# Seven products instead of the plain second product for the third pair of batch 0, with the sums of w2 made earlier

## The chip, the cores and the metric

The kernel runs on one core of one Trainium2 chip. The metric is the device time of one execution in microseconds, given as the median of several runs. Lower is better.

## The reference

Four batches, eight heads, 768 time steps, 48 channels a head. An outer-product recurrence with a forget gate is followed by a mixer over tokens (low rank 32) and channels (384 to 1536 to 384):

```
f = sigmoid(f_logit)
state = f[t,:,None] * state + outer(k[t], v[t])      # per batch and head
y[t]  = q[t] @ state
x = y with the heads side by side                     # 768 x 384 per batch
u = x + (x^T U V)^T                                   # U 768x32, V 32x768
out = u + relu(u @ w_ch1) @ w_ch2                     # 384x1536, 1536x384
```

All is float32, apart from the weights, which arrive as float64 and are turned into float32 on the chip.

## The kernel before

**Units and batches.** Attention is worked in 16 units: unit `n` is one pair of heads of batch `n // 4` (HP = 4 pairs a batch). The front of a unit prepares its operands: `gates` (transpose L748 on VectorE, sigmoid L849 on ScalarE), `keep` (scan L854 and small operations L859 to L864), `keys` (L748 and L791, into kz), `read_back` (scan L872) and `queries` (L748 and L791, into qT). Its rear uses them: `kept` (transposes of kz on TensorE, L980), `states` (products L1001, copied by ScalarE L1008), `scan` (L1023 on VectorE, copied by GpSimd L1027), `scores` (L953, masked into A by VectorE L966), `read` (products L1039) and `inner` (products with A, L1057, then a copy into x by ScalarE, L1063).

**The mixer.** When a batch's attention is done, its `Mixer` follows: `low_rank` and `added_up` (L184, L197), `mix_blocks` (products L214, and an add of each pair of blocks into x by VectorE), `turn` (transposes of x, L288, copied by L289), then for each of three pairs `a` of token blocks the first products (`ch1`, L300, with a relu L335 into z) and the second products. A pair is two blocks of 128 tokens.

**Second products in two ways.** Batch 0 uses plain ones (`ch2`, L352): for each of the two blocks, 12 products of 384 columns, in four pieces of three, with one add to x by VectorE at the end. The other batches use Winograd's form with seven products of quarters in place of eight: `sums_of` makes four sums of z's quarters on VectorE, and `seven` makes the products in steps 0 to 3 (two, two, two and one product, each of six matmuls of 192 columns, L386), with adds on VectorE. Step 1 multiplies by the second and third sums of w2's quarters, step 2 by the fourth and first, steps 0 and 3 by quarters of w2 themselves. Each step of a batch's last pair takes a tile of two PSUM banks ("big", three of them in turn), which the mix products and the turns also use. The float32 matmuls appear as two records each in the trace.

**The sums of w2.** `quarters` makes four sums once, with VectorE: three in tiles named zw, which hold batch 0's z before, and the fourth over a quarter of w2 itself, which the plain form still needs until batch 0's last second product.

**The order of work.** TensorE's order is the written one all through. Up to the fourth piece of batch 1's second phase the orders of VectorE and ScalarE are the written ones too; instructions that come later in the code are placed by a planner and can stand between these. `add` marks VectorE's adds as urgent. `steps` lists the pieces of attention by unit, and `attention` calls a `Fill` before each piece. `Fill` spreads a list of (cost, piece) evenly over a number of portions:

```
self.due += self.share
while self.pieces and self.pieces[0][0] / 2 <= self.due:
    cost, piece = self.pieces.pop(0)
    self.due -= cost
    piece()
```

The attention of batch 1 (from unit 5's `keep` on, 35 pieces) is filled with batch 0's second products of pairs 0 and 1, 16 plain pieces of equal cost. The pieces are, in order: keep 6, keys 6, two steps to (read 4, states 5, scan 5), read_back 6, queries 6, three steps to (inner 4, scores 5, kept 6), gates, keep and keys 7, two to (read 5, states 6, scan 6), three to (inner 5, scores 6, kept 7), read_back and queries 7, gates, keep and keys 8, two to (read 6, states 7, scan 7), three to (inner 6, scores 7, kept 8), read_back and queries 8, gates, keep and keys 9, two to (read 7, states 8, scan 8), inner 7.

`start_mixer(1, ...)` then mixes the second products of pair 2 into batch 1's mixer, in quarters of `after`: a quarter, `low_rank`, unit 9's read_back and queries, a quarter, `added_up`, a quarter, unit 10's gates and keep, `mix_blocks`, a quarter, the turns. The four sums of w2 follow, and then batch 1's first products.

Of the kernel before, what the change touches and what calls it, by code (L numbers as in the profile page):

```python
# [59 lines left out]
def weight_loader(nc, pool, dma):  # L60
# [5 lines left out]

    P = nc.NUM_PARTITIONS

    def load(dst, w, place=None):
# [9 lines left out]
        def start():  # L79
            raw = pool.tile([P, WP], U64, name="w_raw", bufs=RAW) if place is None else place()  # L80
            raw = T["raw"] = raw[0:rows, 0:n]
            dma.dma_start(out=shaped(raw), in_=w)

        def halves():
            y = pool.tile([P, WP], U32, name="w_y")[0:rows, 0:n]
            r = pool.tile([P, WP], I32, name="w_r", bufs=3)[0:rows, 0:n]
            words = T["raw"].bitcast(U32).rearrange("p (n two) -> p n two", two=2)
            lo, hi = words[:, :, 0], words[:, :, 1]

            f = y.bitcast(F32)  # L90
# [52 lines left out]
def by_rows(V, w, R):  # L143


    P, n = V.shape[0], w.shape[1] // V.shape[0]
    G = P // R
    return [
# [8 lines left out]
class Mixer:  # L157
# [6 lines left out]
    def __init__(self, tc, b, x, U, V, w1, w2, sums, ident, blocks, out, two, three, zp, ps_big, ps_mm, wide=False,  # L164
                 z_all=None, room=None, pair=0):
        nc = tc.nc
        P = nc.NUM_PARTITIONS
# [4 lines left out]
        NA = NCH // 2  # L172
        NI = NFC // 2
        HM = DM // 2
# [26 lines left out]
        def add(*args):  # L201

            with tc.high_priority(offset=AHEAD):
                nc.vector.tensor_tensor(*args)  # L204
# [18 lines left out]
        def mix_four():  # L223
            big = ps_big.tile([P, 2, 512], F32, name="pu", tag="big")
            pms = [big[:, s, :] for s in range(2)] + [ps_mm.tile([P, 512], F32, name="pu1", tag="mm") for _ in range(2)]
            for t, pm in enumerate(pms):
                mix_product(pm[:, 0:DM], t)
            add(x[:, 0:2, :], x[:, 0:2, :], big[:, :, 0:DM], ALU.add)
            for t in range(2, NG):
                add(x[:, t, :], x[:, t, :], pms[t][:, 0:DM], ALU.add)  # L230

        def mix_blocks():
            first = 0
            if b > 1 and sums is not None:
                mix_four()
                first = NG
            for t in range(first, NCH):
                mix(t)
# [120 lines left out]
        def part(a, r, c):  # L359
            return z[a, c][:, :, r * P : (r + 1) * P]  # L360

        def sums_of(a):
            for i in range(1, 5):
                if room and a >= pair and (a - pair) % 2 == 0:
                    s = room["S"][i - 1]
                else:
                    s = two.tile([P, WP], U64, name="w_raw", bufs=RAW).bitcast(F32)
                S[a, i] = s.rearrange("p (i t) -> p i t", t=P)
            add(S[a, 1], part(a, 1, 0), part(a, 1, 1), ALU.add)
            add(S[a, 2], S[a, 1], part(a, 0, 0), ALU.subtract)  # L370
            add(S[a, 3], part(a, 0, 0), part(a, 1, 0), ALU.subtract)
            add(S[a, 4], part(a, 0, 1), S[a, 2], ALU.subtract)

        W = {}

        def products(a, parts, *of):

            if 0 in parts:
                if a == NA - 1 and (not room or room["last"] == a - pair):
                    W["pm"] = ps_big.tile([P, 2, 512], F32, name="pw", tag="big")[:, 0]  # L380
                else:
                    W["pm"] = ps_mm.tile([P, 512], F32, name="pw", tag="mm")
            for n in parts:
                lhs, rhs = of[n]
                for i in range(NI):
                    nc.tensor.matmul(W["pm"][:, n * HM : (n + 1) * HM], lhsT=lhs[:, i, :], rhs=rhs[:, i, :],  # L386
                                     start=(i == 0), stop=(i == NI - 1))
            return W["pm"] if len(of) - 1 in parts else None

# [53 lines left out]
        def fewer(a):  # L443
# [51 lines left out]

            return [(FG * P * len(PRODUCTS[k : k + 2]), lambda k=k: two_of(k)) for k in range(0, len(PRODUCTS), 2)]

        def second(a):
            if sums is None:
                return [(2 * NFC * DM // NQ, lambda s=s, n=n: ch2(a, s, n)) for s in range(2) for n in range(NQ)]  # L500
            return [(2 * NFC * HM * (2 if step < 3 else 1) // 2, lambda step=step: seven(a, step))
                    for step in range(4)]

        def halved(a):

            if sums is None:
                return second(a)
            return [(NFC * HM, lambda step=step, n=n: seven(a, step, (n,)))
                    for step in range(4) for n in range(2 if step < 3 else 1)]

        def ready(a):
            return [] if sums is None else [(1, lambda: sums_of(a))]

        def first(a):
            return [(4 * NDC * 2 * P, lambda j=j: ch1(a, j)) for j in range(NI)]
# [5 lines left out]


        self.firsts = [p for j in range(NI) for a in range(NA) for p in [first(a)[j]]]
        self.seconds = [p for a in range(NA) for p in second(a)]
        self.main = first(0)
        for a in range(NA - 1):
            ahead = first(a + 1)
# [5 lines left out]
        self.sums_of_x = lambda a: [(1, lambda: sums_of_x(a))]  # L533


def quarters(nc, pool, w2):


    P = nc.NUM_PARTITIONS
    NI, HM = w2.shape[1] // 2, w2.shape[2] // 2  # L540
    q = {(i, j): w2[:, i * NI : (i + 1) * NI, j * HM : (j + 1) * HM] for i in range(2) for j in range(2)}
    sums = {4: q[0, 1]}
    sub = nc.vector.tensor_tensor

    def place():
        for i in range(1, 4):
            t = pool.tile([P, NI, 2 * P], F32, name="zw")
            sums[i] = t.rearrange("p i t -> p (i t)")[:, 0 : NI * HM].rearrange("p (i d) -> p i d", d=HM)

    return sums, [  # L550
        place,
        lambda: sub(sums[1], q[0, 1], q[0, 0], ALU.subtract),
        lambda: sub(sums[2], q[1, 1], sums[1], ALU.subtract),
        lambda: sub(sums[3], q[1, 1], q[0, 1], ALU.subtract),
        lambda: sub(sums[4], q[1, 0], sums[2], ALU.subtract),
    ]


def factored_path(ctx, tc, q, k, v, f_logit, moe_U, moe_V, moe_w_ch1, moe_w_ch2, out, ok):
# [4 lines left out]
    nc = tc.nc  # L564
    B, H, S, D = q.shape
    P = nc.NUM_PARTITIONS
# [3 lines left out]
    NBL = S // P  # L570
# [9 lines left out]
    W = TB * NB  # L580
# [35 lines left out]
    w1 = const.tile([P, NDC, FF], F32, name="w1")  # L616
    w2 = const.tile([P, NFC, DM], F32, name="w2")
# [99 lines left out]
    U = const.tile([P, NBL, R], F32, name="U")  # L717
    V = const.tile([P, (NBL * R + P - 1) // P, P], F32, name="V")
# [8 lines left out]
    def place():  # L727
        if not spare:
            t = zp.tile([P, NFC // 2, 2 * P], F32, name="zw").rearrange("p i t -> p (i t)").bitcast(U64)
            spare.extend([t[:, 0:WP], t[:, WP : 2 * WP]])  # L730
        return spare.pop(0)
# [3 lines left out]
        take_in(w1[:, :, i * P : (i + 1) * P], w1_rows[:, :, i * P : (i + 1) * P], place if i < FIRST else None)  # L735
        for i in range(NFC)
    ]
    sums, to_sum = quarters(nc, zp, w2)
    weights += [take_in(w2[:, i, :], moe_w_ch2[i * P : (i + 1) * P, :]) for i in range(NFC)]

    def backwards(t, first, n):
# [140 lines left out]
    x_tiles = {}  # L882

    def mixer(b):
        return Mixer(tc, b, x_tiles[b], U, V, w1, w2, sums if b else None, ident, blocks, out, two, three, zp, ps_big, ps_mm,
                     b == 0, z_all, room if b >= B - 2 else None, FEWER - (b - B + 2) * NCH // 4)


# [41 lines left out]
    plain = {n for of in PRODUCTS for _, n in of if n < 9}  # L930
# [222 lines left out]
    with tc.manual_schedule(engines={nc.vector.engine, nc.scalar.engine}):  # L1153
# [65 lines left out]
        m = mixer(0)  # L1219
# [35 lines left out]
        second = chain(front(HP, "gates", "keep", "keys", "read_back", "queries"), steps(HP, 2 * HP + 1))  # L1255
# [6 lines left out]
                next(second)()  # L1262
        for f in loads:
            f()
        n = len(m.seconds) // (NBL // 2)
        todo, after = m.seconds[:-n], m.seconds[-n:]

        attention(second, Fill(todo, 10 + 10 * HP - (len(start) + len(m.firsts) - 1 - EARLY)))
        n = 2 * HP + 2
        m = start_mixer(1, after, front(n - 1, "read_back", "queries"), front(n, "gates", "keep"))  # L1270
        for f in to_sum:
            f()
        pieces, fill = steps(n - 1, 3 * HP + 1), Fill(m.main, 10 * HP - 3)
        for _ in range(4):
            fill()
# [1 line left out]
    for b in range(2, B - 1):  # L1277
        if b > 2:
            pieces, fill = steps(b * HP + 1, (b + 1) * HP + 1), Fill(m.main, 10 * HP)
        after = m.after  # L1280
        attention(pieces, fill)
        m = start_mixer(b, after)
# [7 lines left out]
    todo = m.first(0) + m.ready(0) + m.halved(0)  # L1290
# [14 lines left out]
    todo = of(0, "sums_of_x") + of(0, "fewer")  # L1305
# [359 lines left out]
```

## Time and profile before

| | |
|---|---|
| median of three runs | 468.49 us (468.22 to 468.52) |
| the profiled execution | 467.36 us, span 465.5 us |
| granted TensorE clock | 0.998 |
| busy TensorE, VectorE, ScalarE, GpSimd | 455.7, 352.7, 165.8, 54.4 us |
| plain second products (L352), first to last start | 98.9 to 164.3 us |
| batch 0's pair 2, first to last record (L352) | 145.1 to 164.8 us |
| the four sums of w2 (L552 to L555) | 165.3 to 170.6 us |

A matmul's row in the profile gives its own duration, which overlaps its neighbours'; what a run of matmuls costs is read from the start of one group to the start of the next. VectorE's instructions overlap by less than 0.1 us. In the timelines a bracket gives the idle time ahead of an instruction and what ended it.

### The profile page before, as it was taken

How to read it: one execution, taken by the hardware profiler on the slowest of the kernel's cores; microseconds unless marked ns; L12 is line 12 of the kernel's file. 1: busy time of each engine (PE TensorE's matmuls, PEld its weight loads, DVE VectorE, ACT ScalarE, POOL GpSimd, SP SyncE). 2: the span in 40 equal slices, each digit the busy share in tenths (PEclk: the TensorE clock that was granted, in tenths of full speed). 3: DMA queues.
4: the chain of work that ended last, by engine and by line, in shares of the span. 5: the costliest groups of instructions: out<-in, count | busy, mean ns of one | idle time of the engine just before them, and what ended most of it. 6: DMA issues, size and time to landing. Idle time of an engine off the chain costs nothing.

```text
span 465.5 us, 13015 instructions
## 1 busy us (share of the span) xinstructions
PE 455.7 (98%) x5639; PEld 395.0 (85%) x5639; DVE 352.7 (76%) x581; ACT 165.8 (36%) x316; POOL 54.4 (12%) x60
## 2 busy tenths in 40 slices
PE   8999999999999999999999999999999999999996
PEld 6886888875666578999898888989989999999996
DVE  5777788979999676865774659977797877858642
ACT  6775776562333143323323223331412311112200
POOL 2002445634112001010001000020000000000000
PEclk9999999999999999999999999999999999999999
DMA  9948997577778504505534020100000000001001
GB/s 198 204 115 208 224 218 178 153 115 106 122 112 133 91 18 53 77 3 97 66 52 80 15 52 9 21 5 20 18 1 1 35 1 35 0 1 37 0 36 39
DMA packets 148343, 34.35 MB, mean 74 GB/s; under 512 B 136822, under 2 KB 146742, under 8 KB 148278
## 3 DMA queue, kind: packets, MB, share of 16 engines
q1 hardware_dynamic: 147478, 33.29, 36.2%
q8 instruction: 46, 0.75, 0.7%
q10 hardware_dynamic: 800, 0.15, 0.2%
q14 instruction: 19, 0.16, 0.1%
HBM read 28.70 MB, written 4.72 MB: 72 GB/s over the span
## 4 chain that ended last, share of the span: by engine, by line
PE 79%; DVE 12%; ACT 3%; issue 3%; DMA 2%; POOL 0%; SPq 0%; DVEq 0%; ACTq 0%; POOLq 0%
PE pw L386 25%; PE pz L300 21%; PE pp L489 12%; PE po L352 5%; PE y L1039 2%; PE y L1057 2%; PE sc L953 2%; PE pt L771 2%; PE ds L1001 1%; PE pt L817 1%; DVE late L854 1%; PE pt L980 1%; DVE late L907 1%; PE put L288 1%; PE idle L1160 1%
## 5 line engine op out<-in xcount | busy, mean ns | idle before, releaser
L300 PE MATMUL pz<-uT,w 128*128 128x256 f32 x492 | 111.5, 382 | 0.3
L300 PEld LDWEIGHTS pz<-uT,w 128*128 128x128 f32 x492 | 91.7, 190 | 12.9 <-ACT uT L289 0.6
L1027 POOL COPY st<-added 128x576 f32<-128x576 f32 x12 | 18.2, 1515 | 187.5 <-DVE added L1023 187.5
L386 PE MATMUL pw<-zw,w_raw 128*128 128x192 f32 x216 | 38.0, 329 | 0.0
L386 PE MATMUL pw<-w,z_all 128*128 128x192 f32 x216 | 37.3, 327 | 0.0
L101 POOL TENSOR_TENSOR w<-w_y,w_r 128x384 int32<-128x384 int32 x24 | 31.6, 1317 | 39.5 <-DVE w_y L100 23.3
L386 PEld LDWEIGHTS pw<-w,z_all 128*128 128x128 f32 x216 | 35.3, 190 | 0.5
L335 ACT ACTIVATE z_all<-pz 128x512 f32<-128x512 f32 x33 | 19.6, 597 | 44.9 <-PE pz L300 44.4
L386 PEld LDWEIGHTS pw<-zw,w_raw 128*128 128x128 f32 x216 | 35.1, 190 | 0.6 <-issue 0.3
L854 DVE TENSOR_TENSOR_SCAN late<-fz,late 128x768 f32<-128x768 f32 x12 | 21.1, 1755 | 7.3 <-ACT fz L849 7.1
L482 ACT ACTIVATE other<-other 128x512 f32<-128x512 f32 x18 | 11.3, 631 | 40.3 <-DVE other L204 40.3
L352 PE MATMUL po<-w,zw 128*128 128x384 f32 x72 | 25.2, 495 | 0.0
L352 PE MATMUL po<-w,z_all 128*128 128x384 f32 x72 | 24.7, 493 | 0.0
L872 DVE TENSOR_TENSOR_SCAN late<-fz,other 128x768 f32<-128x768 f32 x12 | 22.0, 1834 | 0.2
L966 DVE TENSOR_TENSOR A<-sc,causal 128x768 f32<-128x768 f32 x16 | 15.2, 951 | 8.9 <-PE sc L953 8.9
L352 PEld LDWEIGHTS po<-w,zw 128*128 128x128 f32 x72 | 13.2, 190 | 9.6 <-issue 0.8
L352 PEld LDWEIGHTS po<-w,z_all 128*128 128x128 f32 x72 | 13.3, 190 | 8.9 <-DVE o L204 0.6
L482 ACT ACTIVATE z_all<-z_all 128x512 f32<-128x512 f32 x12 | 7.6, 630 | 34.1 <-DVE z_all L204 34.1
L1008 ACT COPY added<-ds 48x576 f32<-48x576 f32 (+1 forms) x28 | 17.8, 635 | 5.0 <-PE ds L1001 4.7
L489 PE MATMUL pp<-v_nat,late 128*128 128x128 f32 x152 | 19.1, 275 | 0.0
L1039 PEld LDWEIGHTS y<-st,qT 48*64 48x64 f32 x704 | 13.6, 137 | 6.4 <-issue 3.9
L98 DVE TENSOR_SCALAR w_y<-w_y 128x384 f32<-128x384 f32 (+3 forms) x27 | 12.2, 451 | 8.9 <-ACT w_y L91 8.7
(226 smaller groups left out, 867.7 us busy)
## 6 DMA issues: line engine op xcount, KB each, us to landing
w_raw<-in_moe_w_ch_dram SPq DMA_DIRECT2D x18, 384.0 KB, 3.5
out_dram<-o SPq DMA_DIRECT2D x24, 192.0 KB, 1.9
v_nat<-in_v_dram SPq DMA_DIRECT2D x16, 144.0 KB, 3.4
v_nat<-in_v_dram SPq DMA_DIRECT2D x32, 72.0 KB, 3.3
zw<-in_moe_w_ch_dram SPq DMA_DIRECT2D x6, 384.0 KB, 4.7
w<-in_k_dram SPq DMA_DIRECT2D x4, 288.0 KB, 3.9
w<-in_q_dram SPq DMA_DIRECT2D x4, 288.0 KB, 4.1
late<-in_f_logit_dram SPq DMA_DIRECT2D x10, 96.0 KB, 2.7
```

The costliest lines, as they stand in the source:

```text
L101: nc.gpsimd.tensor_tensor(dst.bitcast(I32), shaped(y.bitcast(I32)), shaped(r), ALU.add)
L300: nc.tensor.matmul(pm[:, i * 2 * P : (i + 1) * 2 * P], lhsT=w1[:, m, o : o + P], rhs=uT[a][:, m, :], start=(m == 0), stop=(m == NDC - 1))
L335: nc.scalar.activation(z[a, c][:, k : k + 2, :].rearrange("p i t -> p (i t)"), pm, AF.Relu)
L352: nc.tensor.matmul(pm, lhsT=z[a, i // NI][:, i % NI, s * P : (s + 1) * P], rhs=w2[:, i, :], start=(i == 0), stop=(i == NFC - 1))
L386: nc.tensor.matmul(W["pm"][:, n * HM : (n + 1) * HM], lhsT=lhs[:, i, :], rhs=rhs[:, i, :], start=(i == 0), stop=(i == NI - 1))
L482: nc.scalar.activation(dst, dst, AF.Relu, scale=float(SIGNS[n]))
L489: nc.tensor.matmul(pm[:, i, r * P : (r + 1) * P], lhsT=room["w"](wn)[:, r * P : (r + 1) * P], rhs=x_node(a, xn), start=((xn, wn) == of[0]) ...
L854: nc.vector.tensor_tensor_scan(backwards(X, S - 1, S), backwards(f, S, S), backwards(ends, S - 1, S), 0.0, ALU.mult, ALU.add,)
L872: nc.vector.tensor_tensor_scan(Y, f[:, 0:S], starts, 0.0, ALU.mult, ALU.add)
L1008: nc.scalar.copy(added[r, 1:].rearrange("p (e c s) -> p e c s", c=NBL, s=2), ds[r, :, 0 : NBL * D].rearrange("p s (c e) -> p e c s", e=D),)
L1027: nc.gpsimd.tensor_copy(st, states.rearrange(by_e, c=NCH))
L1039: nc.tensor.matmul(o(c % 2, par, c // 2), lhsT=T["q"][rows[par], chunk[c]], rhs=T["st"][rows[par], c, :], start=(c <= 2), stop=False, skip ...
```

## The change

Batch 0's third pair (`a` = 2) takes `sums_of` and `seven`; pairs 0 and 1 stay plain (`plain`). The sums of w2 are made in three portions inside the filling of batch 1's attention. The first sum and the third follow pair 0's eight plain pieces; the first lies in the zw tile that pair 0 has freed, the third in three pieces in the integer tiles (w_r) that the conversion of the weights has left. The sums of z for pair 2 follow three pieces of pair 1. The second sum, in the zw tile that pair 1 has freed, and the fourth come after all of pair 1. In `start_mixer` each quarter of `after` is then one step of `seven`, in place of two plain pieces, and the four sums behind it are gone.

```diff
-            if b > 1 and sums is not None:
+            if b > 1:
...
-                    nc.tensor.matmul(W["pm"][:, n * HM : (n + 1) * HM], lhsT=lhs[:, i, :], rhs=rhs[:, i, :],
+                    nc.tensor.matmul(W["pm"][:, n * HM : (n + 1) * HM], lhsT=lhs[:, i, :],
+                                     rhs=rhs[i] if isinstance(rhs, list) else rhs[:, i, :],
...
+        def plain(a):
+            return sums is None or wide and a < NA - 1
+
         def second(a):
-            if sums is None:
+            if plain(a):
                 return [(2 * NFC * DM // NQ, lambda s=s, n=n: ch2(a, s, n)) for s in range(2) for n in range(NQ)]
...
         def ready(a):
-            return [] if sums is None else [(1, lambda: sums_of(a))]
+            return [] if plain(a) else [(1, lambda: sums_of(a))]
...
-    def place():
-        for i in range(1, 4):
-            t = pool.tile([P, NI, 2 * P], F32, name="zw")
-            sums[i] = t.rearrange("p i t -> p (i t)")[:, 0 : NI * HM].rearrange("p (i d) -> p i d", d=HM)
-
-    return sums, [
-        place,
-        lambda: sub(sums[1], q[0, 1], q[0, 0], ALU.subtract),
-        lambda: sub(sums[2], q[1, 1], sums[1], ALU.subtract),
-        lambda: sub(sums[3], q[1, 1], q[0, 1], ALU.subtract),
-        lambda: sub(sums[4], q[1, 0], sums[2], ALU.subtract),
-    ]
+    def place(i):
+        t = pool.tile([w2.shape[0], NI, 2 * w2.shape[0]], F32, name="zw")
+        sums[i] = t.rearrange("p i t -> p (i t)")[:, 0 : NI * HM].rearrange("p (i d) -> p i d", d=HM)
+
+    def first():
+        place(1)
+        sub(sums[1], q[0, 1], q[0, 0], ALU.subtract)
+
+    def third():
+
+        sums[3] = []
+        for i in range(0, NI, 2):
+            t = two.tile([w2.shape[0], WP], I32, name="w_r", bufs=3).bitcast(F32).rearrange("p (i d) -> p i d", d=HM)
+            sub(t, q[1, 1][:, i : i + 2, :], q[0, 1][:, i : i + 2, :], ALU.subtract)
+            sums[3] += [t[:, k, :] for k in range(2)]
+
+    def others():
+        place(2)
+        sub(sums[2], q[1, 1], sums[1], ALU.subtract)
+        sub(sums[4], q[1, 0], sums[2], ALU.subtract)
+
+    return sums, first, third, others
...
-        n = len(m.seconds) // (NBL // 2)
-        todo, after = m.seconds[:-n], m.seconds[-n:]
+        first, third, others = to_sum
+        todo = m.second(0) + [(0, first), (0, third)] + m.second(1)[:3] + m.ready(2) + m.second(1)[3:] + [(0, others)]
+        after = m.after
...
-        for f in to_sum:
-            f()
```

More of the change, by code (lines that the diff above doesn't have):

```diff
@@ L504, in halved @@
         def halved(a):
-            if sums is None:
+            if plain(a):
                 return second(a)
@@ L523, in __init__ @@
         self.firsts = [p for j in range(NI) for a in range(NA) for p in [first(a)[j]]]
-        self.seconds = [p for a in range(NA) for p in second(a)]
         self.main = first(0)
@@ L533, in __init__, with quarters @@
         self.sums_of_x = lambda a: [(1, lambda: sums_of_x(a))]
-def quarters(nc, pool, w2):
-    P = nc.NUM_PARTITIONS
+def quarters(nc, pool, two, w2):
     NI, HM = w2.shape[1] // 2, w2.shape[2] // 2
@@ L737, in factored_path @@
     ]
-    sums, to_sum = quarters(nc, zp, w2)
+    sums, *to_sum = quarters(nc, zp, two, w2)
     weights += [take_in(w2[:, i, :], moe_w_ch2[i * P : (i + 1) * P, :]) for i in range(NFC)]
@@ L884, in mixer @@
     def mixer(b):
-        return Mixer(tc, b, x_tiles[b], U, V, w1, w2, sums if b else None, ident, blocks, out, two, three, zp, ps_big, ps_mm,
+        return Mixer(tc, b, x_tiles[b], U, V, w1, w2, sums, ident, blocks, out, two, three, zp, ps_big, ps_mm,
                      b == 0, z_all, room if b >= B - 2 else None, FEWER - (b - B + 2) * NCH // 4)
```

## The prediction

> **What bounds the kernel now.** I read the page first, then the busy table by stage, then TensorE's and VectorE's timelines around the change.
>
> The page's engine line, and two lines of the busy table (window; then busy us and instructions of PE, PEld, DVE, ACT, POOL; clock; DMA share; GB/s):
>
> ```profile
> PE 455.7 (98%) x5639; PEld 395.0 (85%) x5639; DVE 352.7 (76%) x581; ACT 165.8 (36%) x316; POOL 54.4 (12%) x60
> ...
> 124.80:151.80 27.00, 26.77 (x417) 16.73 (x417) 24.89 (x31) 7.78 (x15) 3.88 (x3) 1.00 0.75 119
> 151.80:166.20 14.40, 14.25 (x83) 7.90 (x82) 9.43 (x14) 2.28 (x5) 0.00 (x0) 1.00 0.42 67
> ```
>
> TensorE looks like the only bound. But from 124.8 to 151.8 us, the second half of batch 1's attention with batch 0's second products as filling, VectorE is busy 24.89 of 27.0 us; its idle rest is 0.9 us in each unit, where L854 waits for ScalarE's sigmoid (L849), and no other work can slip in, since VectorE's order is the written one here. Only from 151.8 to 166.2 us has it room (9.43 of 14.40).
>
> TensorE's timeline where the two meet (start, us, instruction, in brackets the idle time before it):
>
> ```profile
> 133.48 0.89 PE L953 MATMUL sc<-qT,kz 48*64 48x64 f32 x48
> 134.60 0.59 PE L980 MATMUL pt<-ident,kz 64*128 64x64 f32 x12 [0.23 <-DVE kz L791]
> 135.12 4.14 PE L352 MATMUL po<-w,z_all 128*128 128x384 f32 x12
> ```
>
> The transposes of unit 8 (`kept`) start the moment that VectorE has made its kz. TensorE has no lead there: what VectorE does later, TensorE does later.
>
> VectorE's timeline (batch 1's mixer starts at 145):
>
> ```profile
> 133.50 0.96 DVE L791 TENSOR_TENSOR kz<-kz,late 128x768 f32<-128x768 f32 x1
> 136.09 0.95 DVE L966 TENSOR_TENSOR A<-sc,causal 128x768 f32<-128x768 f32 x1
> 154.48 0.56 DVE L204 TENSOR_TENSOR o<-x,po 128x384 f32<-128x384 f32 x1 [2.66 <-PE po L352]
> 160.84 2.65 DVE L204 TENSOR_TENSOR x<-x,pu 128x768 f32<-128x768 f32 x3
> 165.30 1.35 DVE L552 TENSOR_TENSOR zw<-w 128x1152 f32<-128x1152 f32 x1
> 166.68 1.36 DVE L553 TENSOR_TENSOR zw<-w,zw 128x1152 f32<-128x1152 f32 x1
> ```
>
> The 2.66 us is VectorE's one large reserve. The sums of w2 (L552 to L555, 165.3 to 170.6) come when TensorE has begun the next first products (166.20) and waits for nothing.
>
> [...] from 104 to 148 us VectorE's instructions stand in the code's order, and the 0.9 us waits stay empty. [...]
>
> **TensorE's work.** The plain pair has 24 products of 384 columns, two records each: 48 at 0.339 us (12 in 4.07) are 16.3 us. Seven products are 42 of 192 columns, 84 records; 36 take 5.85 us later (L386), so 84 take 13.8 with starts. Saved: 2.5 us. All of it lies after 145.1, in batch 1's mixer.
>
> **VectorE's work.** Instructions overlap by some 0.08 us, so the four sums take 5.3 us, 1.33 each. First sum: 1.33. Third in three pieces of 384: 3 × 0.49 = 1.47. `sums_of(2)`: four adds of 768, as at 186.14 to 189.75: 3.61. Second and fourth: 2.66. The seven's own nine adds: those at 199.5 to 213, 0.75 + 1.75 + 0.8 + 0.3 = 3.6, for two plain ones (0.46 each). One ScalarE copy (0.3) is hidden: ScalarE is busy 7.78 of 27 us. Stores stay two on SP; no load is added or moved past another. The 5.3 us that leave 165.3 to 170.6 gain nothing: no wait of TensorE there names VectorE.
>
> Where it falls follows from `Fill`: 16 pieces over 35 steps, 0.457 a step. The first and third sums come out at step 18, behind A of unit 6 (ends 124.83) and ahead of unit 7's L872. `sums_of(2)` comes at step 25, behind scan 7 (L1023). The others come at the end, behind scan 8.
>
> **The walk.** (1) First and third make VectorE 2.80 us late from 124.83. kz of unit 8 is late by that, and `kept` starts at 137.40 for 134.60: **TensorE waits 2.80**. Everything queued behind it (16 plain pieces' rest, `read`, `inner`) moves along; `inner` of unit 7 ends at 145.13 + 2.80 = 147.93.
>
> (2) `sums_of(2)` makes VectorE 6.41 us late. Next to need it is `inner` 7, with A at 136.95 + 6.41 = 143.36; TensorE comes at 147.1: hidden. Scan 8 ends at 154.64, the others then run to 155.97 (second) and 157.30 (fourth).
>
> (3) TensorE does step 0 of the seven, 3.9 us to 151.85, and `low_rank`, 1.1, to 152.96. Step 1 multiplies by the second sum: 155.97. **It waits 3.0 us**, and `added_up` and step 2 queue behind it: step 1 to 160.0, `added_up` 160.65, step 2 to 164.55, the mix products to 166.05.
>
> (4) VectorE after the others: step 0's adds to 158.05, unit 9's read and queries (3.5) to 161.55, step 1's adds to 163.3, a wait for step 2 (164.55), its adds to 165.35. Then gates and keep of unit 10, 4.2 us with the sigmoid (154.96 to 159.17 now): 169.55. Only then x's three adds, to 172.2. Step 3 needs a two-bank PSUM tile; of the three, the next in turn holds the first mix product, until 170.5. TensorE has been free since 166.05: **it waits 4.45 us**. Step 3 ends at 172.5, turns take 1.48 as now, and L300 starts at 174.0 instead of 166.20.
>
> Sum: 2.80 + 3.0 + 4.45 − 2.45 = +7.8 us. VectorE's account agrees: ahead of the end of x's adds come 2.80 + 3.61 + 2.66 + 3.3, less 0.46, less 1.67 for unit 10's L872 (159.17), which stands ahead of x's adds today but is called later and which I take to move back, less the 2.66 reserve, plus the new 1.25 wait: 163.4 becomes 172.2. After 174 TensorE's work is unchanged and was never waiting for VectorE between 166 and 205, so nothing is won back.
>
> The profiled execution took 467.36 us (span 465.5), 1.13 below the median 468.49. 467.36 + 7.8 = 475.2; against the median **476.3**.
>
> **Unknown costs.** The place of unit 10's L872: at 0 if behind x's adds (taken, as x's operands will have lain ready), +1.67 if ahead: 478.0. The third sum's pieces into the integer tiles: between 1.33 (one instruction's price) and 3 × 0.56 = 1.67; I take 1.47. The other edits cost nothing: `b > 1` alone selects the same batches here, and a list of views in place of one tile changes no instruction's size. The semaphores of the three new waits aren't shown one by one; 0.14 us lies between kz's end and L980's start now, so I allow 0 to 0.5 each. With the work of the adds read 1 us too high or too low, the likeliest case covers 474 to 478.5.
>
> **Rivals.**
> A, *faster*: VectorE's lateness never reaches TensorE, and the 2.45 us stand: 466.0. It decides if kz of unit 8 and the second sum are no later than TensorE's arrival, that is if the sums run in VectorE's idle time, such as the 2.66 us. For it: 5.0 of the 14.4 us from 151.8 on are free on VectorE. Against: 0.23 us of wait at `kept` today, and the written order.
> B, *two waits*: x's adds, marked urgent, go ahead of gates and keep 10; they'd run from 166.05, step 3 from 167, L300 from 170.5: +4.3, 472.8. For it: L872 at 159.17 shows that some instructions are placed out of call order. Against: today gates and keep stand ahead of x's adds.
> C, *one large wait*: the fourth sum overwrites a quarter of w2 whose rows step 0 reads in other columns. If that counted as a conflict, step 0 would wait to 157.35 and the same walk gives L300 at 180.3: +14.1, 482.6. Against: at 40.42 L184 reads columns 288 to 383 of x before VectorE's adds to columns 0 to 287 of the same rows, earlier in the code, begin at 40.80.
>
> **Chances.** The walk 0.76, A 0.09, B 0.10, C 0.03, no effect 0.02. A measurement of this kernel tells about 0.2% (0.9 us) from no change. The range, 471.5 to 480.5, takes in the walk with its unknowns and B; A and C stay outside. Faster 0.09, same 0.02, slower 0.89.
>
> **What would show it.** L980 of unit 8 near 137.4 behind kz (step 1); A of unit 7 near 143.4 with no wait at L1057 (step 2); L386 waiting some 3 us for a zw sum (step 3), then some 4.5 us for x's add (step 4); L300 of batch 1 near 174. The prediction is wrong if L980 of unit 8 stays near 134.6, if the sums stand elsewhere in VectorE's order, or if TensorE, late at 174, ends on time.

## The result, and the profile after

The changed kernel takes 478.74 us (median of six runs, 477.55 to 479.51) against 468.22 us for the kernel before on the same chip: 1.0226 times as long, 95% interval 1.0211 to 1.0240, or 10.5 us. The prediction was 476.3 us, 7.8 us more. The profiled execution took 477.55 us (span 475.7).

The page's engine line; behind it the busy table by stage (columns as in the prediction), where the last window holds what is left of batch 0's pair 2.

```profile
PE 456.8 (96%) x5675; PEld 402.0 (84%) x5675; DVE 360.2 (76%) x594; ACT 166.0 (35%) x317; POOL 54.6 (11%) x60
```

```profile
124.80:151.80 27.00, 23.24 (x393) 15.56 (x392) 24.93 (x32) 6.97 (x14) 1.77 (x1) 0.94 0.51 80
151.80:166.20 14.40, 13.34 (x91) 11.28 (x89) 13.30 (x18) 1.28 (x3) 2.18 (x1) 1.00 0.67 104
166.20:177.00 10.80, 6.53 (x54) 5.56 (x55) 8.65 (x12) 2.29 (x4) 0.00 (x0) 0.84 0.31 64
```

VectorE was busy 24.89 of 27 us in the first window before, and is so still (24.93); what was added is pushed to the right, and TensorE, now idle there for 3.8 us, is pushed with it. From 151.8 to 166.2 VectorE goes from 9.43 to 13.30 of 14.40 us. The 0.94 and 0.84 are granted clocks: 1.00 before.

TensorE's timeline after (start, us, instruction, idle time before it):

```profile
137.07 0.90 PE L992 MATMUL pt<-ident,kz 64*128 64x64 f32 x12 [2.57 <-DVE kz L803]
137.91 5.40 PE L352 MATMUL po<-w,z_all 128*128 128x384 f32 x12
...
149.48 0.92 PE L1069 MATMUL y<-v_nat,A 64*64 64x48 f32 x48 [0.94 <-ACT seen L1058]
...
156.65 2.19 PE L386 MATMUL pw<-zw,w_raw 128*128 128x192 f32 x12 [1.05 <-DVE zw L565]
...
171.23 3.87 PE L386 MATMUL pw<-w,w_raw 128*128 128x192 f32 x12 [3.98 <-DVE x L204]
...
176.51 5.45 PE L300 MATMUL pz<-uT,w 128*128 128x256 f32 x24
```

L992 is what L980 was, L1069 what L1057 was (twelve lines were added). Unit 8's transposes, which waited 0.23 us before, wait 2.57. Batch 1's first products (L300) begin 10.3 us later than before (166.20). From there on nothing more is lost or won: L300 to the end is 299.2 us, and was 299.3.

VectorE's timeline after, at the places the prediction named:

```profile
124.63 1.35 DVE L553 TENSOR_TENSOR zw<-w 128x1152 f32<-128x1152 f32 x1
125.89 1.49 DVE L560 TENSOR_TENSOR w_r<-w 128x384 f32<-128x384 f32 x3
...
135.97 0.96 DVE L803 TENSOR_TENSOR kz<-kz,late 128x768 f32<-128x768 f32 x1
...
139.08 1.84 DVE L204 TENSOR_TENSOR w_raw<-w_raw,z_all 128x768 f32<-128x768 f32 x1
...
143.04 0.94 DVE L978 TENSOR_TENSOR A<-sc,causal 128x768 f32<-128x768 f32 x1
...
155.18 1.33 DVE L565 TENSOR_TENSOR zw<-w,zw 128x1152 f32<-128x1152 f32 x1
156.54 2.24 DVE L566 TENSOR_TENSOR w<-w,zw 128x1152 f32<-128x1152 f32 x1
...
165.37 0.55 DVE L204 TENSOR_TENSOR o<-o,pw 128x384 f32<-128x384 f32 x1 [0.90 <-PE pw L386]
...
170.23 2.67 DVE L204 TENSOR_TENSOR x<-x,pu 128x768 f32<-128x768 f32 x3
```

kz of unit 8 moves from 133.50 to 135.97 and x's adds from 160.84 to 170.23. The sums stand in the order that was read from `Fill`. The line at 165.37 is the first of step 2's adds: VectorE waits 0.90 us for TensorE there, so by then it has worked off what was added.

A measure for the experiments is the **stretch** from the first L352 to batch 1's first L300: 67.1 us before, 77.6 after. The start of pair 2's second products parts it in two (145.13 before, 150.32 after): 5.4 us are lost ahead of it and 5.1 from there to L300. The stretch is cleaner than the whole time: the traces reach the first L352 at 98.7 to 103.5 us, and most of that difference comes from TensorE pauses in the first 45 us that the profile puts down to nothing but "issue".

### The profile page after: what moved, and what is told of

Its sections match the earlier page's. It is cut to its first block, busy times and chain, and to the rows that moved or that the text cites. A ratio compares the mean times of both kernels' runs of the same rounds, so it can differ in the third digit from the quotient of the medians.

```text
span 475.7 us, 13104 instructions
## 1 busy us (share of the span) xinstructions
PE 456.8 (96%) x5675; PEld 402.0 (84%) x5675; DVE 360.2 (76%) x594; ACT 166.0 (35%) x317; POOL 54.6 (11%) x60
## 4 chain that ended last, share of the span: by engine, by line
PE 70%; DVE 18%; issue 4%; ACT 4%; DMA 2%; SPq 1%; POOL 1%; DVEq 0%; ACTq 0%; POOLq 0%
PE pw L386 27%; PE pz L300 18%; PE pp L490 12%; DVE late L866 2%; PE y L1051 2%; DVE late L884 1%; PE sc L965 1%; DVE w_raw L204 1%; DVE added L1035 1%; PE pt L783 1%; PE pt L829 1%; PE ds L1013 1%; PE y L1069 1%; DVE late L760 1%; DVE kz L760 1%
## 5 line engine op out<-in xcount | busy, mean ns | idle before, releaser
L300 PE MATMUL pz<-uT,w 128*128 128x256 f32 x492 | 111.5, 382 | 0.3
L300 PEld LDWEIGHTS pz<-uT,w 128*128 128x128 f32 x492 | 91.7, 190 | 12.9 <-ACT uT L289 0.6
L1039 POOL COPY st<-added 128x576 f32<-128x576 f32 x12 | 18.4, 1535 | 198.1 <-DVE added L1035 198.1
L386 PE MATMUL pw<-w,z_all 128*128 128x192 f32 x228 | 39.5, 327 | 0.0
L386 PEld LDWEIGHTS pw<-w,z_all 128*128 128x128 f32 x228 | 37.2, 190 | 0.6
L335 ACT ACTIVATE z_all<-pz 128x512 f32<-128x512 f32 x33 | 19.6, 598 | 43.9 <-PE pz L300 43.4
L386 PE MATMUL pw<-zw,w_raw 128*128 128x192 f32 x168 | 30.1, 329 | 1.1 <-DVE zw L565 1.1
L386 PEld LDWEIGHTS pw<-zw,w_raw 128*128 128x128 f32 x168 | 27.3, 190 | 1.9 <-PE ph L184 1.4
L884 DVE TENSOR_TENSOR_SCAN late<-fz,other 128x768 f32<-128x768 f32 x12 | 22.0, 1836 | 0.1
L386 PE MATMUL pw<-w,w_raw 128*128 128x192 f32 x84 | 16.8, 354 | 4.0 <-DVE x L204 4.0
L386 PEld LDWEIGHTS pw<-w,w_raw 128*128 128x128 f32 x84 | 15.2, 209 | 5.2 <-DVE x L204 4.6
L861 ACT ACTIVATE fz<-late 128x756 f32<-128x756 f32 x10 | 8.3, 832 | 31.8 <-DVE late L760 31.8
L386 PE MATMUL pw<-w,other 128*128 128x192 f32 x108 | 18.5, 326 | 0.0
```

The lines of the kernel that those rows point to most:

```text
L300: nc.tensor.matmul(pm[:, i * 2 * P : (i + 1) * 2 * P], lhsT=w1[:, m, o : o + P], rhs=uT[a][:, m, :], start=(m == 0), stop=(m == NDC - 1))
L335: nc.scalar.activation(z[a, c][:, k : k + 2, :].rearrange("p i t -> p (i t)"), pm, AF.Relu)
L884: nc.vector.tensor_tensor_scan(Y, f[:, 0:S], starts, 0.0, ALU.mult, ALU.add)
L1039: nc.gpsimd.tensor_copy(st, states.rearrange(by_e, c=NCH))
```

## The experiments

The theory after the result: what counts is where VectorE's added work stands in its order; the same instructions in another order cost nothing. Its rival: the seven-product form costs too much VectorE work here, in whatever order.

| kernel | median, us | times before (95%) | stretch, us |
|---|---|---|---|
| after | 478.74 | 1.0226 (1.0211 to 1.0240) | 77.6 |
| e1: early sums only | 472.06 | 1.0099 (1.0068 to 1.0130) | 71.5 |
| e2: seven only | 476.56 | 1.0193 (1.0161 to 1.0225) | 76.9 |
| e3: x's adds first | 475.77 | 1.0171 (1.0141 to 1.0201) | 73.6 |
| e4: sums behind kz | 480.70 | 1.0266 (1.0240 to 1.0291) | 78.9 |
| e5: dummy products | 478.24 | 1.0217 (1.0188 to 1.0246) | 77.1 |
| e6: reordered | 483.20 | 1.0325 (1.0298 to 1.0352) | 80.2 |
| e7: e6's order, plain pair | 480.32 | 1.0268 (1.0241 to 1.0295) | 77.4 |
| e8: second order | 469.29 | 1.0027 (1.0015 to 1.0038) | 69.9 |
| e9: e8's order, plain pair | 473.76 | 1.0125 (1.0109 to 1.0142) | 67.4 |
| e10: unit 9's keys later | 469.43 | 1.0028 (1.0012 to 1.0043) | 65.3 |
| e11: unit 11's gates sooner | 470.80 | 1.0058 (1.0042 to 1.0074) | 65.3 |

Each ratio is against runs of the kernel before that were taken beside the experiment (medians 467.40 to 468.29 us); it is worked out from the single runs and is not the quotient of the two medians. The stretch is that of the one profiled execution.

**e1, the early sums alone.** Pair 2 stays plain; the first and third sums are made early, the others behind the mixer.

```diff
-            return sums is None or wide and a < NA - 1
+            return sums is None or wide
-        todo = ... + [(0, first), (0, third)] + m.second(1)[:3] + m.ready(2) + m.second(1)[3:] + [(0, others)]
+        todo = ... + [(0, first), (0, third)] + m.second(1)
...
+        others()
```

> The first and third sums of w2 stand where the change puts them, pair 2 stays plain, and the second and fourth sums follow the mixer as in the kernel before. Theory one (every microsecond that VectorE is late at kz of unit 8 is TensorE's, and TensorE has nothing later to win it back with): L992 of unit 8 waits about 2.6 us and the products behind it run some 1.5 us slower at the lower granted clock; 472 us. Theory two (VectorE's reserve of 2.66 us in the mixer takes it back): 468.2 us.

Measured: 4.1 us above the kernel before beside it (472.06 for 468.01), stretch +4.3. TensorE's timeline of e1:

```profile
137.33 0.59 PE L992 MATMUL pt<-ident,kz 64*128 64x64 f32 x12 [2.57 <-DVE kz L803]
137.85 5.83 PE L352 MATMUL po<-w,z_all 128*128 128x384 f32 x12
```

The 2.57 us wait is the sums' own and is never won back. The transposes behind it still take 0.59 us, but the twelve records after them take 5.83 us instead of 4.14: the granted clock is 1.00 from 137.33 to 137.85 and 0.66 from there to 141.0.

**e2, the seven products alone.** Batch 0's pair 2 takes w2's quarters where sums belong (so its output leaves out w2's sums), and the sums stay behind the mixer.

```diff
-        return Mixer(tc, b, x_tiles[b], U, V, w1, w2, sums, ...
+        return Mixer(tc, b, x_tiles[b], U, V, w1, w2, sums if b else quarters_of_w2, ...
-        todo = ... + [(0, first), (0, third)] + m.second(1)[:3] + m.ready(2) + m.second(1)[3:] + [(0, others)]
+        todo = ... + m.second(1)[:3] + m.ready(2) + m.second(1)[3:]
+        for f in (first, third, others):
+            f()
```

> Pair 2 takes the seven products, with four quarters of w2 in place of its sums (the sums of w2 are left out of batch 0's output), and the four sums are made behind the mixer as in the kernel before. Theory one (VectorE's backlog at x's adds decides): no wait at kz of unit 8 and none for a sum of w2, but 3.6 us of z's sums and 3.3 us of adds still make x's adds late; L300 of batch 1 begins at 170 to 172, 472 to 474 us. Theory two (only the sums of w2 hurt, the seven products keep their gain): L300 at 163.7, 465.8 us.

Measured: stretch +9.8, far over what I expected. TensorE's timeline of e2, then VectorE's (line numbers are one higher than in the changed kernel):

```profile
146.59 1.53 PE L1070 MATMUL y<-v_nat,A 64*64 64x48 f32 x48 [2.52 <-ACT seen L1059]
148.06 4.21 PE L386 MATMUL pw<-w,z_all 128*128 128x192 f32 x12
...
170.35 3.81 PE L386 MATMUL pw<-w,w_raw 128*128 128x192 f32 x12 [3.98 <-DVE x L204]
```

```profile
164.50 0.56 DVE L204 TENSOR_TENSOR o<-o,pw 128x384 f32<-128x384 f32 x1 [2.94 <-PE pw L386]
```

Here z's sums alone make unit 9's gates late; `inner` of unit 7 waits for the ScalarE copy `seen`, which stands behind that gates' sigmoid; step 0 then runs at the low clock (4.21 us, 2.1 otherwise). The wait for x's adds is the 3.98 us of the full change, though the sums of w2 are not in this stretch at all and VectorE has just waited 2.94 us for step 2. So this wait is not lateness that was carried along. It comes from the order: between step 2's adds and x's adds stand unit 10's gates and keep (166.11 to 170.23 in the changed kernel). e1, with plain products, has no wait there.

The two halves (+4.3, +9.8) don't add up to +10.5 because they overlap early on. Up to the start of pair 2, e1 loses 4.3 us, e2 3.4 and the full change 5.4: with TensorE late already from unit 8's transposes, `inner` of unit 7 waits 0.94 us and not 2.52.

**e3, x's adds first.** Unit 10's gates and keep go behind step 3.

```diff
-        pieces = after[:n] + m.before[:1] + early + after[n : 2 * n] + m.before[1:2] + after[2 * n : 3 * n] + late
-        pieces += m.before[2:3] + after[3 * n :] + m.before[3:]
+        pieces = after[:n] + m.before[:1] + early + after[n : 2 * n] + m.before[1:2] + after[2 * n : 3 * n]
+        pieces += m.before[2:3] + after[3 * n :] + late + m.before[3:]
```

> The changed kernel, with gates and keep of unit 10 moved behind the mix and step 3. Theory one (step 3's wait comes from the 4.2 us of unit 10 ahead of x's adds): the 4.0 us wait at L386 goes, its products run at full clock, L300 begins near 172.2 instead of 176.5; 474.4 us. Theory two (VectorE's sum of work is the bound, whatever its order): the wait moves to unit 10's keys or later, 478 us.

TensorE's timeline of e3:

```profile
169.73 2.22 PE L386 MATMUL pw<-w,w_raw 128*128 128x192 f32 x12
...
174.94 5.45 PE L300 MATMUL pz<-uT,w 128*128 128x256 f32 x24 [1.73 <-ACT uT L289]
```

Step 3's wait is gone, and with it the low clock (2.22 us for 3.87). But the turned x, uT, is copied by ScalarE, and its copies now stand behind unit 10's sigmoid: 1.73 us of a new wait. The stretch is 4.1 us shorter than after's. The median moved by 3 us only; in this trace the first L352 came at 101.37 us, 2.5 us later than in after's. What step 3 itself waits for is a PSUM tile that x's first add frees. Giving it another tile would be a second way round this wait; no run tried it.

**e4, the first two sums behind kz of unit 8 and scan 7.**

```diff
-        todo = ... + [(0, first), (0, third)] + m.second(1)[:3] + m.ready(2) + m.second(1)[3:] + [(0, others)]
+        todo = ... + m.second(1)[:3] + [(0, first), (0, third)] + m.ready(2) + m.second(1)[3:] + [(0, others)]
```

> The changed kernel, with the first and third sums behind kz of unit 8 and scan 7. Theory one (VectorE's backlog decides, the early wait is only a part of a later one): the 2.6 us wait at L992 goes, but the second sum is ready at the same time, so step 1 waits 3 to 5 us instead of 1.1; 477.5 to 478.7 us. Theory two (the waits add up): 2.6 us and 1.6 us of lower clock are won, 474.6 us.

TensorE's timeline of e4:

```profile
137.33 0.59 PE L992 MATMUL pt<-ident,kz 64*128 64x64 f32 x12 [0.15 <-DVE kz L803]
...
152.54 1.54 PE L1069 MATMUL y<-v_nat,A 64*64 64x48 f32 x48 [5.31 <-ACT seen L1058]
...
174.79 4.21 PE L386 MATMUL pw<-w,w_raw 128*128 128x192 f32 x12 [3.97 <-DVE x L204]
```

The first wait goes, and comes back twice as long at `inner` of unit 7, through ScalarE: what VectorE owes at that point is the same and only shows elsewhere. Step 1, where I had expected the wait, doesn't wait at all. The wait at the end is 3.97 us again, although VectorE waits 1.37 us for step 2 at 168.94; as in e2 it depends on the order and not on how late VectorE was before.

**e5, dummy products keep TensorE busy** in two of the waits: ten ahead of unit 8's transposes, sixteen ahead of step 3.

```diff
+            if n == 2 * HP:
+                for _ in range(10):
+                    nc.tensor.matmul(pt[:, 0, 0:P], lhsT=ident, rhs=ident, start=True, stop=True)
...
+        pieces += m.before[2:3] + ([(0, keep_clock)] if late else []) + after[3 * n :] + m.before[3:]
```

> The changed kernel, with ten 128 x 128 products of the identity ahead of unit 8's transposes (overwritten by them) and sixteen ahead of step 3 (not read), so that TensorE works in place of waiting. Theory one (the waits cost a second time, since the clock is lowered after them): the products behind the two places run at full clock again; the early place gives nothing, as step 1 waits for the second sum till 156.6 anyway, the late one gives the 1.8 us by which step 3 took 3.9 us; L300 near 174.7, 476.9 us. Theory two (both losses count): 3.3 us, 475.4 us. Theory three (the lower clock has nothing to do with the waits): 478.7 us or more.

TensorE's timeline of e5:

```profile
138.40 4.14 PE L352 MATMUL po<-w,z_all 128*128 128x384 f32 x12
...
151.23 3.86 PE L386 MATMUL pw<-w,z_all 128*128 128x192 f32 x12
...
172.69 2.22 PE L386 MATMUL pw<-w,w_raw 128*128 128x192 f32 x12 [0.21 <-DVE x L204]
```

Both groups run at full speed (4.14 for 5.40, 2.22 for 3.87), and the granted clock is 1.00 from 135.3 to 142.3, where the changed kernel has 0.57 from 137.07 to 141.0. So in this wait it was idleness that brought the lower clock. But only 0.6 us of the stretch is won: TensorE, sooner done with the first group, waits 2.61 us at `inner` of unit 7, step 0 pays the low clock instead, and the turns wait 0.53 us for one of x's adds.

**e6 and e7, a first rearrangement, with seven products and with the plain pair.** Unit 9's gates, keep and keys leave the second phase; with its read_back and queries and unit 10's gates and keep they go behind step 3, ahead of the turns. The filling is spread over 32 portions in place of 35, and in e6 the first sums also come later.

```diff
-            yield from front(n + 1, "gates", "keep", "keys")
+            if n != 2 * HP:
+                yield from front(n + 1, "gates", "keep", "keys")
...
+        pieces = after[:n] + m.before[:1] + after[n : 2 * n] + m.before[1:2] + after[2 * n : 3 * n]
+        pieces += m.before[2:3] + after[3 * n :] + early + late + m.before[3:]
```

> The changed kernel with VectorE's order rearranged: first and third sums and z's sums behind A of unit 7; the whole front of unit 9 and the gates and keep of unit 10 behind the mix and step 3; 32 portions of filling in place of 35, since three pieces of the attention have left it. Theory one (the loss is VectorE's order at three places, the seven products save what they should): no wait at unit 8's transposes, at inner of unit 7, at step 1 or step 3; L300 of batch 1 at 163.9 instead of 166.2 in the kernel before; 466 us. Theory two (VectorE's sum of work from 104 to 200 us is too much in any order): the wait appears at unit 9's transposes or at unit 10's, 469 to 474 us.

> The kernel before (plain pair 2, the four sums behind the mixer) with the same rearrangement of unit 9's and unit 10's fronts and of the filling. If the gain of the rearranged kernel is that of the seven products, this one stays at 468 us within 0.7; if the order alone gives it, this one falls to 466 as well; if unit 9's front comes too late behind the 5.3 us of sums, it rises to 470.

TensorE's timeline of e6, then of e7:

```profile
183.63 7.27 PE L300 MATMUL pz<-uT,w 128*128 128x256 f32 x24 [11.28 <-ACT uT L289]
```

```profile
176.62 6.98 PE L300 MATMUL pz<-uT,w 128*128 128x256 f32 x24 [11.47 <-ACT uT L289]
```

My expectations for both failed (466, and 466 to 470), by the mistake that e2 and e3 had already shown: uT's copies stand on ScalarE behind unit 10's sigmoid, which needs all that VectorE was given to do first. In e6 that sigmoid waits 8.60 us for VectorE and starts at 181.94, and the copies follow at 182.79. Step 1 also waits 2.38 us for the second sum in e6. e7 pays about the same wait for uT (11.47 us for 11.28) with plain products, so that wait belongs to this order, not to the seven.

**e8 and e9, a second rearrangement.** Unit 8's read_back and queries, unit 9's gates, scan 8 and unit 9's keep and keys, in this order, go to the start of batch 1's mixer; unit 10's gates, unit 9's read_back and queries and unit 10's keep go behind the turns; the first sums come after six pieces of pair 1, and the filling has 30 portions. e9 has the same order of attention, with the plain pair and the sums where they were before.

```diff
+            held = n == 2 * HP
...
-        todo = m.second(0) + [(0, first), (0, third)] + m.second(1)[:3] + m.ready(2) + m.second(1)[3:] + [(0, others)]
+        todo = m.second(0) + m.second(1)[:6] + [(0, first), (0, third)] + m.second(1)[6:7] + m.ready(2) + m.second(1)[7:] + [(0, others)]
...
-        m = start_mixer(1, after, front(n - 1, "read_back", "queries"), front(n, "gates", "keep"))
+        ahead_of = front(n - 2, "read_back", "queries") + front(n - 1, "gates") + rear(n - 2, "scan") + front(n - 1, "keep", "keys")
+        behind_of = front(n, "gates") + front(n - 1, "read_back", "queries") + front(n, "keep")
+        m = start_mixer(1, after, ahead_of, behind_of)
```

> The seven products for pair 2 with a second arrangement: unit 8's read_back and queries and unit 9's front leave the attention and stand ahead of step 0 and behind the sums of w2, ScalarE's copies of that unit go ahead of unit 9's sigmoid, the first and third sums and z's sums stand behind kz of unit 8, unit 10's gates and keep and unit 9's read_back and queries stand behind the turns and so behind ScalarE's copies of uT; 30 portions of filling. Theory one (the loss is only in what stands ahead of what on VectorE and ScalarE, the seven products save 2.5 us of TensorE): no wait over 0.5 us from the first plain product (L352) to the first L300 of batch 1; that stretch takes 65.6 us, against 67.1 before and 77.6 in the changed kernel; 466 to 467.5 us. Theory two (VectorE has too much work in this stretch in any order): waits of 2 us or more remain, 470 us and more.

> The kernel before (plain pair 2, four sums behind the mixer) with the same second arrangement. The order alone gives nothing if TensorE was the bound all through the stretch: it takes 67.1 us again, 468 us; then the difference to the kernel with the seven products is their own gain. If this one gains as well, the gain is the order's.

TensorE's timeline of e8, then of e9:

```profile
160.79 1.48 PE L214 MATMUL pu<-h,V 32*128 32x384 f32 x8 [0.44 <-DVE o L204]
163.03 1.59 PE L214 MATMUL pu<-h,V 32*128 32x384 f32 x4 [0.77 <-DVE w_y L204]
164.56 4.21 PE L386 MATMUL pw<-w,w_raw 128*128 128x192 f32 x12
```

```profile
191.56 10.65 PE L300 MATMUL pz<-uT,w 128*128 128x256 f32 x36 [3.67 <-ACT z_all L335]
```

For most of the loss the theory holds: order alone takes it from 2.26% to 0.27%, some 9 of the 10.5 us. The trace doesn't reach the 65.6 us of stretch that I expected: step 0's adds still stand behind unit 9's keys, the mix products wait twice, and step 3 runs at the low clock. This profiled execution (471.43 us) was the longest of the 22, though. Nine of them had a granted clock of 0.998 or more and took 467.25 to 468.92 us; the other thirteen had 0.993 to 0.996 and took 469.19 to 471.43. So step 3's low clock may not come in every execution: the middles of the two groups lie 1.7 us apart, and twelve records that take 4.21 us in place of 2.1 would account for that. It isn't shown, as only one of these executions was profiled.

In the same order the plain pair is 4.5 us slower, where I had expected 468: with w2's sums still behind the mixer (from 172.37 us on), unit 9's scan comes late, ScalarE's copy L990 waits 8.19 us for it, and a relu (L335) stands behind that copy. So the seven products together with the early sums gain within this order, though not over the kernel before. How much is the products' part and how much that of the early sums, e9 doesn't tell, since it changes both.

**e10, one move more**: unit 9's keep and keys behind x's adds.

```diff
-        ahead_of = front(n - 2, "read_back", "queries") + front(n - 1, "gates") + rear(n - 2, "scan") + front(n - 1, "keep", "keys")
-        behind_of = front(n, "gates") + front(n - 1, "read_back", "queries") + front(n, "keep")
+        ahead_of = front(n - 2, "read_back", "queries") + front(n - 1, "gates") + rear(n - 2, "scan")
+        behind_of = front(n, "gates") + front(n - 1, "keep", "keys", "read_back", "queries") + front(n, "keep")
```

> The order of e8_order_two with one more move: keep and keys of unit 9 go from ahead of step 0's sums to behind x's adds (step 0's adds then need not wait for about 4.5 us of keep and keys on VectorE). VectorE's reserve theory: step 0's adds come some 2 to 4 us earlier, the mix products no longer wait (0.44 + 0.77 us in e8), step 3's products run at 2.1 to 2.2 us instead of 4.21, and the stretch from the first L352 to batch 1's L300 is 65 to 66.5 us (before 67.1, e8 69.9): about 466 to 467, at or just under the kernel before. Rival, the load only moves: keep, keys, read_back of unit 9 and keep of unit 10 all come behind x's adds, so kz of unit 9 or ScalarE's uT and relu copies (behind unit 10's sigmoid) are late at or just behind L300, TensorE waits 2 us or more there, and the time is 469 or more.

TensorE's timeline of e10, then ScalarE's:

```profile
160.95 2.22 PE L386 MATMUL pw<-w,w_raw 128*128 128x192 f32 x12
164.59 5.45 PE L300 MATMUL pz<-uT,w 128*128 128x256 f32 x24
...
180.15 7.13 PE L300 MATMUL pz<-uT,w 128*128 128x256 f32 x24 [1.98 <-ACT z_all L335]
```

```profile
178.78 0.83 ACT L861 ACTIVATE fz<-late 128x756 f32<-128x756 f32 x1 [5.89 <-DVE late L760]
179.51 0.58 ACT L335 ACTIVATE z_all<-pz 128x512 f32<-128x512 f32 x1
```

Both theories are half right. The stretch is 65.3 us, 1.8 shorter than before, which is nearly all that the seven products save: from start to start they take 14.2 us here, and the plain pair took 16.2. Then it is given back. The relu stands behind unit 11's sigmoid, whose transpose VectorE reaches only at 177.75; L300 waits 1.98 us, and 24 records take 7.13 us instead of 5.45: 3.7 us in all, and L300 to the end is 303.0 us for 299.3.

**e11, unit 11's gates ahead of unit 10's keep.**

```diff
+            if n == 2 * HP + 1:
+                yield from joined(front(n + 2, "gates") + front(n + 1, "keep", "keys"))
```

> The order of e10 with keep of unit 10 behind instead of ahead of unit 11's gates (and those ahead of unit 10's read_back), so that ScalarE's sigmoid of unit 11 comes some 4 to 5 us sooner and no longer stands late ahead of the relu (L335) that L300 waited 1.98 us for in e10. ScalarE-order theory: that wait goes, the 24 products after it take 5.45 us instead of 7.13, the stretch stays at 65 to 66 us and what follows L300 returns from 303.0 to about 299.3: some 465.5 to 466.5, 0.3 to 0.5% under the kernel before. Rival, VectorE's backlog is the cause and only shows elsewhere: keep, keys and read_back of unit 10 come 1 us later, and TensorE then waits for kz or for the state at the next L992 or L1051 by as much; 468 to 469.5 again.

TensorE's timeline of e11, then ScalarE's, and the busy tables of e11 and of before for 26 us from about 2.5 us ahead of L300 on (VectorE's is the third pair of figures):

```profile
177.98 5.45 PE L300 MATMUL pz<-uT,w 128*128 128x256 f32 x24
...
188.09 10.96 PE L300 MATMUL pz<-uT,w 128*128 128x256 f32 x36 [2.58 <-ACT z_all L335]
```

```profile
186.74 0.67 ACT L1002 COPY whole<-whole 128x576 f32<-128x576 f32 x1 [7.28 <-DVE added L1035]
187.44 0.60 ACT L335 ACTIVATE z_all<-pz 128x512 f32<-128x512 f32 x1
```

```profile
162.00:188.00 26.00, 23.36 (x375) 19.90 (x373) 24.59 (x33) 10.31 (x19) 1.16 (x1) 0.99 0.60 83
```

```profile
163.50:189.50 26.00, 25.85 (x383) 21.62 (x383) 20.05 (x22) 11.34 (x19) 1.21 (x1) 1.00 0.26 43
```

e10's wait is gone, and the next relu waits: it stands behind a copy (L1002) that needs unit 9's scan, which VectorE ends at 186.7. So the rival is right in kind, though it named other places (kz or the state) and a shorter time (468 to 469.5): VectorE has 24.59 us of work where the kernel before gives it 20.05, and in e10 and e11 the move only chose which ScalarE instruction was late. No order tried here beats the kernel before. That none can is not shown.

## Why the prediction was right, and where it was off

The prediction had the direction and its three waits right, each behind the instruction it named. The time was 2.7 us more than its sum: it lacked a fourth wait and the slower products behind two of the waits.

**Step 1, the wait at `kept`: right.** Predicted L980 (now L992) at 137.40, measured 137.07; first and third sums 2.67 us for 2.80 (the third's price, 0.49 us a piece, was my estimate: before, the 384-column add of 154.48 took 0.56 us, 0.48 to the next start; the three pieces took 1.49 us for the predicted 1.47). The prediction left out the price behind the wait: the transposes took 0.90 us instead of 0.59 and the twelve records of L352 5.40 instead of 4.14. e1 shows wait and after-effect by themselves.

**Step 2, "hidden": wrong in part.** A of unit 7 was done at 143.9, predicted 143.36, and no product waited for A. But `inner` of unit 7 also waits for ScalarE's `seen`. ScalarE's timeline before, then after:

```profile
144.01 0.16 ACT L1046 COPY seen<-y 128x2 f32<-128x2 f32 x1 [1.58 <-PE y L1039]
```

```profile
148.44 0.83 ACT L861 ACTIVATE fz<-late 128x756 f32<-128x756 f32 x1 [9.00 <-DVE late L760]
149.29 0.14 ACT L1058 COPY seen<-y 128x2 f32<-128x2 f32 x1
```

Before, the copy waited for TensorE only. Now the 0.14 us copy stands behind unit 9's sigmoid, which waits 9.00 us for VectorE's transpose. VectorE's lateness thus reaches TensorE through an engine that is 35% busy. The price was a wait of 0.94 us here, and of 2.5 to 5.3 us in e2, e4 and e5. I had counted ScalarE as cover because it has time; what counts is its order.

**Step 3, the wait for the second sum: right in its place, wrong in its size.** Step 1 began at 156.65, predicted 155.97. The wait was 1.05 us, not 3.0, because TensorE was late too: lower clock and `seen`. That these two losses, which the prediction lacked, cost nothing in the end is luck: they ran inside a wait that was there for another reason. The same holds for the saving, which was put at 2.45 us and is 1.9 (14.2 us from start to start, not 13.8, against 16.2).

**Step 4, the wait for x's adds: right.** 3.98 us for 4.45, step 3 at 171.23 for 170.5; unit 10's L884 (the old L872) did fall behind x's adds, as taken. The **mis-sized term** is what follows: step 3 and turns were put at 3.5 us and took 5.3, as step 3's twelve records took 3.87 us instead of 2.1 at the lower clock. That is 1.8 of the 2.5 us by which L300 came later than 174.0. The other 0.7 us came in with the second sum: one of z's sums ahead of it, priced from instructions that ran alone, stood beside a GpSimd copy (L1039). GpSimd's timeline after:

```profile
138.33 1.77 POOL L1039 COPY st<-added 128x576 f32<-128x576 f32 x1 [13.58 <-DVE added L1035]
...
155.39 2.18 POOL L1039 COPY st<-added 128x576 f32<-128x576 f32 x1 [15.29 <-DVE added L1035]
```

The add at 139.08 took 1.84 us instead of 0.96, and 0.2 us of that was made up, as the program reached the stretch 0.2 us sooner. L566 at 156.54 took 2.24 us instead of 1.36, but this cost nothing: VectorE waits 0.90 us for step 2 behind it.

**Rivals.** A (faster) is refuted by the four waits. B (two waits, x's adds first) did not occur; e3 made it occur, and its +4.3 was +6.5; the rival's sum lacked the low clock behind the first wait, the wait for `seen` and uT's wait. C (fourth sum in conflict with step 0) did not occur: step 0 waited for nothing of L566.

What stays open: the pauses named "issue" in the first 45 us. They differ from trace to trace, and as each program was profiled once, whether they belong to the program or to the execution isn't shown.

## What to carry to other kernels

When an engine other than the bound is nearly full in a stretch, price added work there at the next instruction of the bound that waits for it, then follow every in-order queue between the two: a short copy behind a late sigmoid passes the lateness on. Tell lateness that is carried along from a wait that the order makes anew: if the late engine itself waited just before (0.90 us at 165.37 here), giving it less to do earlier won't help (e2), and moving what stands between does (e3). Count the slower products behind a wait of TensorE too (here they followed each single wait of 1.98 us or more in and behind the stretch, and cost 1.5 to 3.2 us more), and test a form that saves work in the order that suits it before giving the form up. A delay that was moved, as in e10 and e11, is not gone until the engine that owes the work has an idle stretch to do it in.

## What the hardware showed

**TensorE's clock after a wait.** In and behind the stretch, single waits of 0.94 to 1.73 us left the next products at their speed (2.19 us for twelve records of 192 columns after 1.05). Waits from 1.98 us on slowed them: 7.13 for 5.45 us after 1.98, 5.40 for 4.14 after 2.57, 10.96 for 8.04 after 2.58, 3.87 for 2.1 after 3.98. In the changed kernel the granted clock was 0.57 from 137.07 to 141.0, behind the 2.57, and 0.55 from 171.23 to 175.03, behind the 3.98. The slowest groups of twelve took 4.21 us (e2, e4, e8), twice the 2.1 of a group at a clock of 1.00. In e5, dummy products in place of the first of these waits kept the clock at 1.00. Length alone doesn't decide: in e8 two short waits, 0.44 and 0.77 us, came ahead of a step 3 at 4.21 us. Near 38 us both e4 and e9 have two pauses of 0.84 and 0.41 us; the 48 products (L1069, in e9 L1057) that start 1.7 and 1.3 us behind the second pause took 1.53 us in e4 (granted clock 0.55 from 39.6 to 43.4) and 0.92 in e9 (1.00). What else decides is not shown.

**VectorE beside GpSimd.** Twice in the changed kernel both engines took longer side by side. The copy of 138.33 took 1.77 us and ended at 140.10; the add that began at 139.08 took 1.84 us instead of 0.96 and ended at 140.92, 0.82 us after it. At 155.39 the copy began during L565 and took 2.18 us, where those of 194.74 to 264.65 take 1.21 to 1.22; L566 behind L565 took 2.24 us instead of 1.36. Why, the trace doesn't show.
